# Products with the values on the two column halves of the array, each head with its own probabilities

## The chip, the core and the metric

The kernel runs on one core of a Trainium2 chip. The metric is device time in microseconds (us) from one launch to its end; lower is better. Before the change three runs gave 427.7, 428.08 and 429.15 us, median 428.08 us.

The core has TensorE (PE in the rows, with PEld for its weight loads), VectorE (DVE), ScalarE (ACT), GpSimd (POOL) and SyncE (SP), which issues the transfers. They run at the same time and wait for each other by semaphores.

## What is computed

The reference is attention with four sink positions and a window of 128, then two layers; the second layer's experts are only touched by tokens with a positive skip score.

```python
# q, k, v: 2 batches x 8 heads x 768 positions x 64
scores = scale * np.matmul(q, k.transpose(0, 1, 3, 2))
scores = np.where(is_sink | in_window, scores, -1e9)
a = np.exp(scores - scores.max(-1, keepdims=True))
a = a / (a.sum(-1, keepdims=True) + 1e-09)
x = np.matmul(a, v)               # 1536 tokens x 512, the products with the values
h = x @ w_in                      # 512 x 2048
g = np.where(h >= 1, h, np.where(h <= -1, 0, (h + 1) ** 2 / 4))
x = g @ w_out                     # 2048 x 512; then the skip layer
```

## The kernel before, in words

Work on attention goes by pairs of heads: 2 batches x 3 groups of 256 positions (`g` = 0, 1, 2) x 4 pairs of heads, so 24 pairs. A pair passes through these steps, each a function of the kernel: `trans_q` and `trans_k` (transposes of queries and keys), `score` (products of queries and keys, maximum on VectorE, exponential on ScalarE), `norm` (division by the sum), `ptrans` (the probabilities are transposed, 128x128 blocks, and copied to the tile `pth`, one half for each head, by ScalarE at L421), `ptrans_sinks` (the same for the sinks' probabilities, copied to `psk` by ScalarE at L430) and `av`, the products with the values.

`score` works with 64 rows of TensorE's array for each head (L366): the two heads' operands lie on partitions 0 to 63 and 64 to 127, and their results go to two banks of PSUM. All other matmuls before the change use the whole array.

`av` (L432 to L458) takes a block of 128 keys at a time. The stationary operand is 128 keys x 128 columns, the 64 columns of both heads side by side. The moving operand is the probabilities of both heads one after the other, up to 2 x 256 columns. So the result has, for each head's probabilities, the product with both heads' values, and half of it is used: rows 0 to 63 of the first 256 columns, and rows 64 to 127 of the second 256. These products are in full fp32, which the trace shows as two passes for each matmul. A pair with `g` = 0 has two such matmuls (512 and 256 columns), the others three (512, 256 and 256 columns) and one for the sinks from `psk` (512 columns, in the reduced format fp32r, one pass). Then ScalarE copies each head's half to `xh` (L456) and VectorE takes the rest into `xl` (L457), so that `xh` + `xl` hold the result for the fp32r matmuls that follow.

The first layer (`h_mm` at L471, `h_act`, `y_mm` at L516) begins while attention still runs: its matmuls are cut into pieces, and TensorE's order is written out by hand in the loop at L668. In each step a string such as `..a..A...Ps` sets it: a dot stands for pieces of the layer, `a` and `b` for scores, `P` and `s` for the transposes of probabilities, `A` for `av`. The order of VectorE's and ScalarE's instructions in this part is set by a scheduler when the program is built. Weights come in as raw words through SP and are converted on VectorE and ScalarE (L175 to L186) in the same stretch. After the last pair the rest of the layer runs (`behind`, L553), with everything ordered by hand, and then a short end that reads the skip scores.

Of the kernel before, what the change touches and what calls it, by code (L numbers as in the profile page):

```python
# [8 lines left out]
F32 = mybir.dt.float32  # L9
# [3 lines left out]
AF = mybir.ActivationFunctionType  # L13
ALU = mybir.AluOpType
# [10 lines left out]
def attention_moe_skip_kernel(  # L25
# [15 lines left out]
    nc = tc.nc  # L41
    B, H, S, D = q.shape
    NT, DM = out.shape
    DFF = w_in.shape[1]
    P = 128
# [53 lines left out]
    for i in range(2):  # L99
        a, b = mask[i][:, 0:P], mask[i][:, P + SK:]  # L100
# [4 lines left out]
    xh = [xp.tile([P, KC, 256], F32R, name=f"xh{g}") for g in range(NGRP)]  # L105
    xl = [xp.tile([P, KC, 256], F32R, name=f"xl{g}") for g in range(NGRP)]
# [9 lines left out]
    vall = ap.tile([P, 3, H, D], F32, name="vall", bufs=1)  # L116
# [5 lines left out]
    psk = ap.tile([P, 256], F32R, name="psk", bufs=1)  # L122


    kst, vsk = {}, {}
# [144 lines left out]
    def geo(n):  # L270

        b, g, h = units[n]
        return b, g, h, ([2 * g + 1, 2 * g] if g % 2 else [2 * g, 2 * g + 1]), (0 if g % 2 else 1)
# [158 lines left out]
    def av(u):  # L432
        b, g, h, _, _ = geo(2 * u)
        o = pst.tile([P, 512], F32, name="pt")


        oj = o.rearrange("p (j c) -> p j c", j=2)

        if g == 0:
            mm = [(1, 0, 256, 0), (2, 128, 128, 2)]  # L440
        else:
            mm = [(1, 0, 256, 0), (2 if g % 2 else 0, 0, 128, 2), (0 if g % 2 else 2, 128, 128, 3)]
        todo = []
        pth = pr_[u]["pth"]
        for kb, c0, w, i0 in mm:
            vs = vall[:, kb, h:h + 2].rearrange("p j d -> p (j d)")
            todo.append((oj[:, :, c0:c0 + w], vs, pth[:, :, i0 * P:i0 * P + w]))
        if g:
            todo.append((oj, vsk[b][:, h // 2], psk[0:72].unsqueeze(1).to_broadcast([72, 2, 256])))
        for i, (out_, lhs, rhs) in enumerate(todo):  # L450
            nc.tensor.matmul(out_, lhs, rhs, start=(i == 0), stop=(i == len(todo) - 1))  # L451
        gi = b * NG + g
        hp = h // 2
        for j in range(2):
            r = slice(D * j, D * j + D)
            nc.scalar.activation(xh[gi][r, hp], oj[r, j], AF.Copy)  # L456
            nc.vector.tensor_tensor(out=xl[gi][r, hp], in0=oj[r, j], in1=xh[gi][r, hp].bitcast(F32), op=ALU.subtract)  # L457
        pr_[u] = None  # L458


# [206 lines left out]
    with tc.manual_schedule(engines={mybir.EngineType.PE}):  # L667
        for s_ in range(-1, NU + 1):  # L668
# [26 lines left out]
            for what in order:  # L695
                if what == ".":
                    a, b = np_ * dot // dots, np_ * (dot + 1) // dots
                    dot += 1
                    for i in range(b - a):
                        pieces[done["piece"]]()  # L700
                        done["piece"] += 1
                elif what == "q":
                    upto("tq", done["tq"] + 1, NPR, trans_q)
                elif what == "k":
                    upto("tk", done["tk"] + 1, NPR, trans_k)
                elif what == "a" and s_ // 2 + 1 < NPR:
                    score(s_ // 2 + 1, 0)
                elif what == "b" and (s_ + 1) // 2 < NPR:
                    score((s_ + 1) // 2, 1)
                    norm((s_ + 1) // 2)  # L710
                elif what == "P":
                    upto("p", s_ + (s_ >= LAG), NU, ptrans)
                elif what == "s":
                    upto("ps", (s_ + (s_ >= LAG)) // 2, NPR, ptrans_sinks)
                elif what == "A":
                    upto("av", before // 2, NPR, av)
# [252 lines left out]
    todo = const.tile([P, NTT + 1], F32, name="todo")  # L969
# [45 lines left out]
```

## Time and profile before

| | |
|---|---|
| runs shown | 427.7, 428.08, 429.15 us |
| time of the profiled execution | 428.26 us |
| its span on the core | 426.4 us |
| mean granted clock of TensorE | 0.975 of full speed |
| busy: TensorE, its weight loads | 394.9 us (93%), 327.1 us (77%) |
| busy: VectorE, ScalarE, GpSimd | 267.0 us (63%), 231.5 us (54%), 30.5 us (7%) |
| moved by DMA | 53.29 MB, 125 GB/s on average |

The span runs from the first to the last instruction of the program; the execution's own time is 1.86 us longer. Busy time is an average over stretches with different limits, so the rows further down are taken stretch by stretch. A matmul's record lasts from its start to the modelled end of its results, which lies after the next matmul's start: the time that one takes of TensorE is the distance to the next start, not the length of its record.

### The profile page before, as it was taken

What the parts mean: (1) busy time and instruction counts of PE and PEld (TensorE: products, weight loads), DVE (VectorE), ACT (ScalarE), POOL (GpSimd) and SP (SyncE); (2) the same over time, 40 slices, a digit from 0 to 9 for tenths busy, and PEclk for the clock granted to TensorE, in tenths of its full rate; (3) what the DMA queues carried; (4) which work ended last, traced back from release to release, by engine and by line L of the source; (5) the groups of instructions that cost most, each with busy time, mean ns of one, the idle gap of its engine ahead of it and who ended that gap; (6) DMA issues with size and microseconds to landing.
All of it is one profiled execution on the core that took longest, in us unless ns stands there. A gap on an engine that the chain in (4) does not pass through costs nothing.

```text
span 426.4 us, 6940 instructions
## 1 busy us (share of the span) xinstructions
PE 394.9 (93%) x2420; PEld 327.1 (77%) x2420; DVE 267.0 (63%) x710; ACT 231.5 (54%) x563; POOL 30.5 (7%) x132
## 2 busy tenths in 40 slices
PE   4877869999999999999999899999999999999970
PEld 2544547777787787788789799999999999999960
DVE  1799974445566676555635987887837854444462
ACT  4788976666767676666664554554533333333310
POOL 5111110000001011100100000000000000000000
PEclk9988989999999999999999999999999999999995
DMA  8787561305033022100100656544435996555131
GB/s 191 193 244 203 160 199 26 73 2 138 10 78 101 16 62 72 53 22 7 49 2 25 198 180 216 148 119 128 141 105 180 312 321 214 184 188 187 48 137 69
DMA packets 65579, 53.29 MB, mean 125 GB/s; under 512 B 40320, under 2 KB 56704, under 8 KB 65536
## 3 DMA queue, kind: packets, MB, share of 16 engines
q1 hardware_dynamic: 64448, 52.51, 41.1%
q8 instruction: 21, 0.34, 0.3%
q10 hardware_dynamic: 1088, 0.26, 0.3%
q14 instruction: 22, 0.18, 0.1%
HBM read 46.47 MB, written 6.29 MB: 124 GB/s over the span
## 4 chain that ended last, share of the span: by engine, by line
PE 83%; DVE 4%; DMA 4%; issue 3%; ACT 2%; SPq 1%; POOL 1%; ACTq 0%; DVEq 0%; POOLq 0%
PE ph L471 20%; PE y L516 18%; PE z L516 11%; PE pt L471 11%; PE pt L451 9%; PE sc L366 5%; PE pt L417 4%; PE pt L304 1%; DMA ext<-in_window_dram 1%; DMA raw<-in_moe_w_in_dram 1%; DVE pr L370 1%; PE pt L331 1%; PE pt L429 1%; DMA out_dram<-mr 1%; DVE mr L539 1%
## 5 line engine op out<-in xcount | busy, mean ns | idle before, releaser
L471 PE MATMUL ph<-xh,wi 128*128 128x256 f32 x496 | 95.2, 290 | 4.2 <-DVE mt L491 3.6
L471 PEld LDWEIGHTS ph<-xh,wi 128*128 128x128 f32 x496 | 77.7, 189 | 9.1 <-DVE mt L491 3.9
L516 PE MATMUL y<-wo,gh 128*128 128x512 f32 x224 | 73.1, 408 | 1.2 <-ACT mr L535 1.2
L471 PE MATMUL ph<-xl,wi 128*128 128x256 f32 x248 | 70.0, 282 | 0.6 <-DVE xl L457 0.6
L374 ACT ACTIVATE pr<-pr,negmax 128x260 f32<-128x260 f32 (+1 forms) x96 | 46.8, 488 | 26.1 <-DVE negmax L370 25.4
L499 DVE TENSOR_TENSOR gl<-mt,gh 128x512 fp32r<-128x512 f32 x48 | 33.2, 692 | 27.5 <-ACT gh L493 27.2
L516 PE MATMUL z<-wo,gh 128*128 128x512 f32 x160 | 49.3, 389 | 0.0
L471 PE MATMUL pt<-xh,wi 128*128 128x256 f32 x272 | 48.8, 281 | 0.0
L493 ACT ACTIVATE gh<-mt 128x512 fp32r<-128x512 f32 x48 | 30.3, 630 | 33.5 <-DVE mt L491 12.2
L471 PEld LDWEIGHTS ph<-xl,wi 128*128 128x128 f32 x248 | 47.5, 192 | 0.8 <-DVE xl L457 0.8
L451 PE MATMUL pt<-pth,vall 128*128 128x256 f32 (+1 forms) x128 | 45.6, 491 | 1.4 <-ACT qtf L307 1.4
L516 PEld LDWEIGHTS y<-wo,gh 128*128 128x128 f32 x224 | 38.5, 189 | 8.0 <-ACT mr L535 1.4
L516 PE MATMUL y<-wo,gl 128*128 128x512 f32 x112 | 43.9, 392 | 0.0
L471 PEld LDWEIGHTS pt<-xh,wi 128*128 128x128 f32 x272 | 42.7, 188 | 1.3
L491 DVE SCALAR_TENSOR_TENSOR mt<-ph,mt 128x512 f32<-128x512 f32 x31 | 21.4, 689 | 28.6 <-ACT mt L486 28.4
L485 ACT ACTIVATE mt<-ph,half 128x512 f32<-128x512 f32 x31 | 21.2, 684 | 31.8 <-PE ph L471 31.6
L471 PE MATMUL pt<-xl,wi 128*128 128x256 f32 x136 | 38.2, 281 | 0.0
L451 PEld LDWEIGHTS pt<-pth,vall 128*128 128x128 f32 x128 | 24.5, 202 | 16.8 <-issue 13.2
L370 DVE CUSTOM_DVE_ANT_0 pr<-sc,mask 128x260 f32<-128x260 f32 x64 | 25.4, 424 | 16.3 <-PE sc L366 16.1
L457 DVE TENSOR_TENSOR xl<-pt,xh 64x256 fp32r<-64x256 f32 x48 | 20.2, 420 | 23.5 <-ACT xh L456 23.0
L516 PEld LDWEIGHTS z<-wo,gh 128*128 128x128 f32 x160 | 28.8, 188 | 4.9
L516 PE MATMUL z<-wo,gl 128*128 128x512 f32 x80 | 31.1, 389 | 0.0
(101 smaller groups left out, 617.0 us busy)
## 6 DMA issues: line engine op xcount, KB each, us to landing
raw<-in_moe_w_in_dram SPq DMA_DIRECT2D x32, 512.0 KB
raw<-in_moe_w_out_dram SPq DMA_DIRECT2D x32, 512.0 KB
vall<-in_v_dram SPq DMA_DIRECT2D x24, 128.0 KB
ypart<-mr SPq DMA_DIRECT2D x12, 256.0 KB
yi<-ypart SPq DMA_DIRECT2D x12, 256.0 KB
out_dram<-mr SPq DMA_DIRECT2D x12, 256.0 KB
qn<-in_q_dram SPq DMA_DIRECT2D x22, 128.0 KB
kn<-in_k_dram SPq DMA_DIRECT2D x22, 128.0 KB
```

The costliest lines, as they stand in the source:

```text
L366: nc.tensor.matmul(scs[j][:, :w], qq[r], kk[r], start=(n == 0), stop=(n == len(parts) - 1))
L370: nc.vector.tensor_tensor_reduce(out=a, in0=scs[j][:, :w], in1=m, scale=-0.125, scalar=BIG, op0=ALU.add, op1=ALU.min, accum_out=negmax[:, ...
L374: nc.scalar.activation(a, a, AF.Exp, bias=negmax[:, mi:mi + 1], scale=-1.0, accum_out=lsum[:, 2 * j + t:2 * j + t + 1])
L417: nc.tensor.transpose(pt[:, P * i:P * i + P], pr[:, t, c:c + P], ident)
L451: nc.tensor.matmul(out_, lhs, rhs, start=(i == 0), stop=(i == len(todo) - 1))
L457: nc.vector.tensor_tensor(out=xl[gi][r, hp], in0=oj[r, j], in1=xh[gi][r, hp].bitcast(F32), op=ALU.subtract)
L471: nc.tensor.matmul(ph, wih[f + i][:, wx, c * P:c * P + P], xx[gi][:, c], start=(c == 0 and x == 0), stop=(c == KC - 1 and x == 2),)
L485: nc.scalar.activation(t, ph, AF.Relu, bias=half, scale=0.5)
L491: nc.vector.scalar_tensor_tensor(out=t, in0=ph, scalar=1.0, in1=t, op0=ALU.max, op1=ALU.min)
L493: nc.scalar.activation(gh, t, AF.Copy)
L499: eng.tensor_tensor(out=gl, in0=t, in1=gh.bitcast(F32), op=ALU.subtract)
L516: nc.tensor.matmul(ycur[gi, tt], gg[:, c:c + P], woh[f + i][:, wx], start=(u == us[0] and i == 0 and x == 0), stop=(u == us[-1] and i == 1 ...
```

## The change

`av` alone changes. The sinks' product comes first, with the whole array and the 256 columns of `psk` once, since both heads' rows of `psk` and of `vsk` lie apart anyway. Each product with a block of keys is cut into two matmuls: the stationary operand is one head's 64 columns, the moving operand that head's probabilities alone, and the result goes to rows 0 to 63 or 64 to 127 of the same 256 columns. Such a matmul uses 64 columns of the array, the first head the left half and the second the right half. One copy on ScalarE and one subtraction on VectorE, both over 128 rows, take the place of two each. After the change `av` is at L443 to L452, and later lines have moved up by five.

```diff
-        oj = o.rearrange("p (j c) -> p j c", j=2)
-
         if g == 0:
             mm = [(1, 0, 256, 0), (2, 128, 128, 2)]
         else:
             mm = [(1, 0, 256, 0), (2 if g % 2 else 0, 0, 128, 2), (0 if g % 2 else 2, 128, 128, 3)]
-        todo = []
         pth = pr_[u]["pth"]
-        for kb, c0, w, i0 in mm:
-            vs = vall[:, kb, h:h + 2].rearrange("p j d -> p (j d)")
-            todo.append((oj[:, :, c0:c0 + w], vs, pth[:, :, i0 * P:i0 * P + w]))
         if g:
-            todo.append((oj, vsk[b][:, h // 2], psk[0:72].unsqueeze(1).to_broadcast([72, 2, 256])))
-        for i, (out_, lhs, rhs) in enumerate(todo):
-            nc.tensor.matmul(out_, lhs, rhs, start=(i == 0), stop=(i == len(todo) - 1))
+            nc.tensor.matmul(o[:, 0:256], vsk[b][:, h // 2], psk[0:72], start=True, stop=False)
+        for i, (kb, c0, w, i0) in enumerate(mm):
+            for j in range(2):
+                nc.tensor.matmul(
+                    o[D * j:D * j + D, c0:c0 + w], vall[:, kb, h + j], pth[:, j, i0 * P:i0 * P + w],
+                    start=(i == 0 and g == 0), stop=(i == len(mm) - 1))
         gi = b * NG + g
         hp = h // 2
-        for j in range(2):
-            r = slice(D * j, D * j + D)
-            nc.scalar.activation(xh[gi][r, hp], oj[r, j], AF.Copy)
-            nc.vector.tensor_tensor(out=xl[gi][r, hp], in0=oj[r, j], in1=xh[gi][r, hp].bitcast(F32), op=ALU.subtract)
+        nc.scalar.activation(xh[gi][:, hp], o[:, 0:256], AF.Copy)
+        nc.vector.tensor_tensor(out=xl[gi][:, hp], in0=o[:, 0:256], in1=xh[gi][:, hp].bitcast(F32), op=ALU.subtract)
```

TensorE's order around a pair with sinks, late in attention, before the change:

```order
L366 MATMUL sc<-kt_145,qt 128x260 x6
L516 MATMUL y_2095<-wo,gh 128x512 x2
L516 MATMUL y_2095<-wo,gl 128x512
L451 MATMUL pt<-pth,vall 128x512
L451 MATMUL pt<-pth,vall 128x2x128 x2
L451 MATMUL pt<-psk,vsk 128x512
L471 MATMUL ph<-xh_128,wi 128x256 x2
L471 MATMUL ph<-xl_134,wi 128x256
```

And after it:

```order
L366 MATMUL sc<-kt_145,qt 128x260 x6
L511 MATMUL y_2105<-wo,gh 128x512 x2
L511 MATMUL y_2105<-wo,gl 128x512
L443 MATMUL pt<-psk,vsk 128x256
L446 MATMUL pt<-pth,vall 64x256 x2
L446 MATMUL pt<-pth,vall 64x128 x4
L466 MATMUL ph<-xh_128,wi 128x256 x2
L466 MATMUL ph<-xl_134,wi 128x256
```

What stands before and behind the pair is the same; the sinks' product moved from the end to the front, and three matmuls over the whole array became six over half of it. Whole-array matmuls stand on both sides.

ScalarE's order at the end of the same part of the program, before the change (`xh` is the copy in question, `psk` the sinks' copy, `mt` and `gh` belong to the layer):

```order
L374 ACTIVATE pr,lsum<-pr,negmax 128x260 x2
L486 ACTIVATE mt<-mt 128x512
L456 ACTIVATE xh_128<-pt 64x256
L493 ACTIVATE gh<-mt 128x512
L456 ACTIVATE xh_128<-pt 64x256
L421 ACTIVATE pth<-pt 128x512
```

And after it:

```order
L374 ACTIVATE pr,lsum<-pr,negmax 128x260 x2
L481 ACTIVATE mt<-mt 128x512
L451 ACTIVATE xh_128<-pt 128x256
L421 ACTIVATE pth<-pt 128x512
L488 ACTIVATE gh<-mt 128x512
```

The second copy is gone, and the copy of the next pair's probabilities has moved ahead of `gh`. Elsewhere too the scheduler has put VectorE's and ScalarE's instructions in another order, most in the first pairs.

## Rows read from the trace of the kernel before

**Rows 1.** Three stretches: length, busy time of PE, PEld, DVE, ACT, POOL, clock, DMA:

```profile
20.00:62.00 42.00, 31.59 (x148) 20.09 (x147) 37.87 (x106) 36.79 (x104) 6.33 (x18) 0.90 0.72 213
62.00:226.00 164.00, 163.40 (x1026) 129.07 (x1026) 92.40 (x319) 106.37 (x302) 16.92 (x78) 0.99 0.18 47
226.00:414.00 188.00, 186.36 (x1201) 169.63 (x1199) 124.59 (x243) 76.29 (x122) 0.00 (x0) 1.00 0.52 168
```

**Rows 2.** Two of these stretches, L451 alone: busy time of PE and PEld:

```profile
20.00:62.00 42.00, 10.06 (x23) 4.50 (x21) 0.90 0.72 213
62.00:226.00 164.00, 38.49 (x121) 22.46 (x121) 0.99 0.18 47
```

**Rows 3.** Timeline of TensorE around one pair with sinks (start us, length us):

```profile
188.09 0.28 PE L471 MATMUL ph<-xh,wi 128*128 128x256 f32 x1
...
188.67 1.88 PE L451 MATMUL pt<-pth,vall 128*128 128x512 f32 x6
...
190.63 0.64 PE L516 MATMUL y<-wo,gh 128*128 128x512 f32 x2
```

**Rows 4.** Timeline of TensorE, single passes of one pair without sinks:

```profile
136.54 0.59 PE L451 MATMUL pt<-pth,vall 128*128 128x512 f32 x1
...
136.97 0.38 PE L451 MATMUL pt<-pth,vall 128*128 128x256 f32 x1
...
137.19 0.38 PE L451 MATMUL pt<-pth,vall 128*128 128x256 f32 x1
```

**Rows 5.** Timeline of TensorE, transposes and a visit of `score` in fp32, in parts:

```profile
30.70 0.49 PE L417 MATMUL pt<-ident,pr 128*128 128x128 f32 x3
...
30.92 0.27 PE L417 MATMUL pt<-ident,pr 128*128 128x128 f32 x1
...
31.12 0.49 PE L366 MATMUL sc<-ktf,qtf 64*128 64x260 f32 x2
...
31.44 0.39 PE L366 MATMUL sc<-ktf,qtf 64*128 64x260 f32 x2
```

**Rows 6.** Timeline of TensorE, a visit whose second head came late:

```profile
33.15 0.48 PE L366 MATMUL sc<-ktf,qtf 64*128 64x260 f32 x1 [0.84 <-DVE negmax L370]
...
33.48 0.51 PE L366 MATMUL sc<-ktf,qtf 64*128 64x260 f32 x2
```

**Rows 7.** Timeline of TensorE, from a visit of `score` to the whole array:

```profile
46.28 0.39 PE L366 MATMUL sc<-ktf,qtf 64*128 64x260 f32 x2
...
46.60 0.50 PE L471 MATMUL ph<-xh,wi 128*128 128x256 f32 x2
...
46.82 0.28 PE L471 MATMUL ph<-xh,wi 128*128 128x256 f32 x1
```

**Rows 8.** Groups by shape, 64 and 128 rows: busy, mean ns of one, idle before:

```profile
L456 ACT ACTIVATE xh<-pt 64x256 fp32r<-64x256 f32 x48 | 18.1, 378 | 17.8 <-PE pt L451 9.7 <-DVE xl L457 7.5
L336 ACT ACTIVATE kt<-pt 128x256 fp32r<-128x256 f32 x12 | 4.5, 374 | 0.0
L457 DVE TENSOR_TENSOR xl<-pt,xh 64x256 fp32r<-64x256 f32 x48 | 20.2, 420 | 23.5 <-ACT xh L456 23.0
L337 DVE TENSOR_TENSOR kt<-pt,kt 128x256 fp32r<-128x256 f32 x12 | 5.1, 421 | 2.7 <-ACT kt L336 2.7
```

**Rows 9.** Timeline of TensorE, its waits between 49 and 60 us:

```profile
50.45 0.50 PE L471 MATMUL ph<-xh,wi 128*128 128x256 f32 x2 [0.57 <-ACT xh L456]
51.51 0.39 PE L471 MATMUL ph<-xl,wi 128*128 128x256 f32 x1 [0.56 <-DVE xl L457]
...
59.26 0.50 PE L471 MATMUL ph<-xh,wi 128*128 128x256 f32 x2 [3.62 <-DVE mt L491]
```

**Rows 10.** Timeline of all engines, the sinks' copy `psk` and the start of `av`:

```profile
187.15 0.37 ACT L430 ACTIVATE psk<-pt 72x256 fp32r<-72x256 f32 x1
...
215.16 0.36 ACT L430 ACTIVATE psk<-pt 72x256 fp32r<-72x256 f32 x1
...
215.36 1.07 PE L451 MATMUL pt<-pth,vall 128*128 128x512 f32 x2
```

## The prediction

> **What bounds the kernel now.** I read busy time by stretches first, since the busy share of the whole span mixes them. From 62 to 226 us, where attention and the first layer are interleaved, TensorE is busy 163.4 of 164 us, ScalarE 106.4 and VectorE 92.4; from 226 to 414 us it is 186.4 of 188. In both TensorE is the bound, and what it is spared shortens the time. From 20 to 62 us it is not: TensorE is busy 31.6 of 42 us, VectorE 37.9, ScalarE 36.8 [rows 1]. The same stretches for line 451 alone tell where the changed products lie: 121 passes between 62 and 226 us [rows 2]. A pair with sinks has seven passes (two for each of three fp32 matmuls, one for the sinks), one without has four, and 15 x 7 + 4 x 4 = 121: 15 pairs with sinks and 4 without lie where TensorE is the bound. The other 5 of the 24 (4 without, 1 with) lie earlier.
>
> Then the timeline, pass by pass. A pass over 512 columns takes 0.43 us (136.54 to 136.97), one over 256 columns 0.22 [rows 4]; so 0.43 for 512, 0.215 for 256 and, in proportion, 0.108 for 128. A pair with sinks goes from 188.67 to the next line's start at 190.63, 1.96 us [rows 3]: two passes at 0.43 and four at 0.215 are 1.72, which leaves 0.24 for the sinks. A pair without them is 2 x 0.43 + 2 x 0.215 = 1.29 us.
>
> **The change, part by part.** *The columns.* Each fp32 product now streams half the columns, but there are twice as many matmuls, so TensorE gains only if the two heads' matmuls run side by side. No row shows two matmuls side by side on column halves. The nearest rows are `score`, which has the two heads on row halves. There the two first passes of the two heads fill 31.12 to 31.61 together and the second passes start at 31.44: each pass pair takes about as long as one pass alone, 0.22 us for 260 columns [rows 5]. I take the same for column halves. Then a pair without sinks streams 2 x (0.215 + 0.108) = 0.645 us, one with sinks 2 x (0.215 + 0.108 + 0.108) = 0.86. The bounds are these and no sharing at all, 1.29 and 1.72 us.
>
> On columns only the skill has a figure: the Trainium skill's page TensorE: Matmul & The Clock Gate (Part 3, Measured speedup vs the span model) gives 2.38 times for three column tiles; an estimate from it, 79% of the ideal, is 1.59 times for two, 1.08 us instead of 0.86, and the whole sum 421 us.
>
> *The sinks.* One pass over 256 columns in fp32r. The layer's passes of that size and format stand 0.12 us apart (five between 188.09 and 188.67 [rows 3]); so 0.12 instead of 0.24.
>
> *Changing between the whole array and halves.* This is what the change adds. Before a visit of `score` the last of three transposes starts at 30.92, and each takes (0.49 - 0.27) / 2 = 0.11 us, so its columns end at 31.03; the second passes start at 31.44, so the first ones' columns began at 31.22. That is 0.19 us with nothing streaming [rows 5]. Leaving a visit, the last passes start at 46.28 and end their columns at 46.50; the next pass but one starts at 46.82, and 0.12 before it, at 46.70, the first one's columns began: 0.20 us [rows 7]. `av` has whole-array matmuls on both sides, as the order shows, and the sinks' product, whole too, stands ahead of the halves, so each of the 24 pairs pays both once: 0.39 us. Column halves may cost less (first weight load of 64 columns) or more; bounds nothing and twice as much. I take the rows as they are.
>
> Sum for TensorE: a pair with sinks 0.12 + 0.39 + 0.86 = 1.37, which is 0.59 less than 1.96. One without 0.39 + 0.645 = 1.03, 0.26 less than 1.29. In the bound stretch 15 x 0.59 + 4 x 0.26 = 9.9 us.
>
> *One copy and one subtraction.* A copy of 64 x 256 takes 378 ns on ScalarE, one of 128 x 256 374; on VectorE 420 and 421 [rows 8]. Twice the rows cost nothing more, so each pair spares 0.38 us of ScalarE and 0.42 of VectorE. From 62 us on this hides behind TensorE and counts as nothing. TensorE's saving needs that cover too: if it takes 9.9 us less for the stretch, about 154 us remain, and ScalarE keeps 106 - 19 x 0.38 = 99 of work in them. Before 62 us the two engines are close to full, and 5 pairs spare VectorE 2.1 us and ScalarE 1.9. TensorE also waits there for exactly these halves, 0.57 us for `xh` and 0.56 for `xl` [rows 9]. But the scheduler has written both engines' order anew in this stretch, and transfers take part in it (DMA busy 0.72). I count half of 2.1, 1.0 us; bounds 2.5 gained (all of it, and a little of the waits) and 3.6 lost (a new wait like the longest there, the 3.62 us at 59.26 [rows 9]).
>
> *A wait moved.* The sinks' product now stands first, so `av` waits for `psk` about 1.7 us sooner; queued behind it are the pair's other products and then the layer's pieces. `psk` was ready at 187.52 for the pair at 188.67, but at 215.52 for the one that began at 215.36 [rows 10, 3]. I count 0.2 us once. The products' own wait for `pth` is the same as before, since ScalarE writes `pth` ahead of `psk`.
>
> The rest of the program is the same work from attention's end on, bound by TensorE, and moves up as a whole. The profiled execution took 428.26 us, 0.2 above the median of the runs shown; 428.26 - 9.9 - 1.0 + 0.2 = 417.6 us.
>
> **The rivals.**
>
> *Side by side, but in the order of the program.* Each fp32 matmul is two passes. If a matmul may not start ahead of one that stands before it, head 1's first pass waits for head 0's second to start, and only these two overlap. Worked through, with passes of 0.215 and 0.108 us, the streams end 0.215 us later in both kinds of pairs (0.86 instead of 0.645, 1.08 instead of 0.86). 19 x 0.215 = 4.1 us are lost: 421.7 us. Against it: in `score` the first two passes start together, so head 1's first pass went ahead of head 0's second [rows 5]; and where head 1 came late, head 0's first pass ran alone and its second shared the array with head 1's first [rows 6]. For it: rows show this for row halves alone. The page named above says in the same Part 3 (What overlaps and what doesn't) that matmuls start and end in strict program order; by that rule this rival would be the forecast, and the two rows on `score` disagree with it.
>
> *No side by side.* Column halves need two different moving operands on all 128 partitions at once; row halves need one on each set of 64, so the rows on `score` do not prove it. If the halves run one after the other, a pair with sinks takes 0.12 + 0.39 + 1.72 = 2.23 us, 0.27 more than before, and one without 0.39 + 1.29 = 1.68, 0.39 more: 15 x 0.27 + 4 x 0.39 = 5.6 us. With the 1.0 spared earlier and the 0.2 added, 433.1 us. It turns slower than before once the two heads share less than about 0.3 of the 1.72 us, which is what the changes of the array and the shorter sinks come to.
>
> *The first stretch gives part of it back.* If the new order on VectorE and ScalarE adds one wait of 3.6 us before 62 us in place of the 1.0 spared, the time is 428.26 - 9.9 + 0.2 + 3.6 = 422.2 us. For it: waits of this size stand in that stretch now. Against it: less work on the two engines that are full there.
>
> **How the numbers follow.** The forecast 0.66, order of the program 0.12, no side by side 0.11, the first stretch 0.11. About 0.3%, 1.3 us, is what can be told from no change. The forecast and the order rival are faster; the first stretch is, but for 0.03, where its waits eat the whole gain; no side by side is slower. So faster 0.86, same 0.03, slower 0.11. The forecast's own range is 414 to 420, from 2.5 us gained before 62 us and somewhat cheaper changes of the array to about 2 lost. With changes of the array that cost nothing 19 x 0.39 = 7.4 us more would be gained, with twice the cost as much lost; part of that, and both faster rivals, set the range at 412 to 425 us. It leaves out the slower case.
>
> **What would show it.** In the changed profile: the two heads' first passes at the new products start within some 10 ns of each other; a pair with sinks takes about 1.37 us from the sinks' start to the next line's start and one without 1.03; TensorE stays above 99% busy until attention ends, now near 215 us; one copy and one subtraction a pair at 0.37 and 0.42 us. The prediction is wrong if head 1's passes begin only when head 0's have ended, if much more than 0.39 us of a pair passes with nothing streaming, or if attention's first part ends later than 62 us.

## The result and the profile after

The changed kernel takes 416.28 us (median of four runs, 414.88 to 417.27), the kernel before 428.21 (427.7 to 429.15): a ratio of 0.971, 95% interval 0.969 to 0.974. Forecast was 417.6 us. The profiled execution took 416.49 us against 428.26, 11.8 us less.

First the stretches. The columns are as in [rows 1]: length, busy time of PE, PEld, DVE, ACT and POOL, clock, DMA. Each boundary lies 0.3 to 0.4 us ahead of the sixth pair's start, 3.3 us behind the last pair's start, and at the end of the layer, as in [rows 1].

```profile
20.00:60.20 40.20, 28.63 (x170) 18.63 (x167) 35.55 (x102) 34.17 (x99) 6.30 (x19) 0.85 0.77 229
60.20:215.20 155.00, 153.69 (x1136) 121.27 (x1136) 84.10 (x301) 98.16 (x283) 16.88 (x78) 0.99 0.20 50
215.20:402.40 187.20, 185.68 (x1197) 169.00 (x1196) 123.81 (x242) 76.17 (x121) 0.00 (x0) 1.00 0.52 168
```

Against [rows 1] the middle stretch is 9.0 us shorter (164.0 to 155.0), and TensorE is still busy for all but 1.3 us of it. The first is 1.8 us shorter, the last 0.8. The middle one ends a fixed time behind the last pair's start, so what the last pair itself gains, some 0.6 us, falls into the last stretch here. The granted clock of the middle stretch is the same 0.99.

Now one pair with sinks on TensorE, in the place of [rows 3]: start, length, then the line. The last three rows are parts of the second `av` row, cut out by narrow windows.

```profile
179.75 0.28 PE L466 MATMUL ph<-xl,wi 128*128 128x256 f32 x1
179.87 0.28 PE L443 MATMUL pt<-psk,vsk 72*128 72x256 f32 x1
180.08 1.09 PE L446 MATMUL pt<-pth,vall 128*64 128x256 f32 x12
181.10 0.73 PE L511 MATMUL y<-wo,gh 128*128 128x512 f32 x2
181.67 0.40 PE L511 MATMUL y<-wo,gl 128*128 128x512 f32 x1
...
180.08 0.44 PE L446 MATMUL pt<-pth,vall 128*64 128x256 f32 x2
...
180.34 0.39 PE L446 MATMUL pt<-pth,vall 128*64 128x256 f32 x2
...
180.56 0.50 PE L446 MATMUL pt<-pth,vall 128*64 128x128 f32 x6
```

Two passes fill 180.08 to 180.52 together, where one takes 0.43; the next two start together at 180.34, and those of 128 columns follow from 180.56. That is the picture of `score` in [rows 5], on columns instead of rows. The 12 passes cover 1.09 us with the tail of the last.

The row behind the pair, and its weight loads (PEld), tell when TensorE really goes on:

```profile
181.10 0.30 PEld L511 LDWEIGHTS y<-wo,gh 128*128 128x128 f32 x2 [0.17 <-issue]
```

The second pass at L511 starts at 181.10 + 0.73 - 0.39 = 181.44 and the one behind it at 181.67, so a pass takes 0.23 us, and the first one's columns began 0.23 before the second's, at 181.21. The second load starts there too (181.10 + 0.30 - 0.19). So the pair takes 1.34 us from the sinks' start (179.87) to 181.21, where it took 1.96. Its parts: sinks 0.12; then nothing streams until 180.13 (0.215 ahead of the second passes at 180.34), 0.14 us; columns until 181.00, 0.87 us; and 0.20 us until 181.21.

On the other engines a copy and a subtraction over 128 rows take what those over 64 took [rows 8], 24 of each in place of 48 (busy, mean ns, idle before):

```profile
L452 DVE TENSOR_TENSOR xl<-pt,xh 128x256 fp32r<-128x256 f32 x24 | 10.1, 420 | 12.1 <-ACT xh L451 12.0
L451 ACT ACTIVATE xh<-pt 128x256 fp32r<-128x256 f32 x24 | 9.0, 376 | 5.3 <-PE pt L446 5.1
```

The waits of TensorE between 47 and 58 us, in the place of those of [rows 9]:

```profile
47.99 0.38 PE L443 MATMUL pt<-psk,vsk 72*128 72x256 f32 x1 [1.25 <-ACT psk L430]
...
57.24 0.50 PE L466 MATMUL ph<-xh,wi 128*128 128x256 f32 x2 [3.21 <-DVE mt L486]
```

The two waits for `xh` and `xl` are gone, the long one for `mt` has stayed, and a new one for `psk` stands ahead of the fifth pair, since the sinks' product now comes first.

### The profile page after: what moved, and what is told of

Read it like the earlier page. It is cut to its first block, busy times and chain, and to the rows that moved or that the text cites. A ratio compares the mean times of both kernels' runs of the same rounds, so it can differ in the third digit from the quotient of the medians.

```text
span 414.7 us, 7132 instructions
## 1 busy us (share of the span) xinstructions
PE 381.2 (92%) x2548; PEld 316.9 (76%) x2548; DVE 255.5 (62%) x686; ACT 220.5 (53%) x539; POOL 30.2 (7%) x132
## 4 chain that ended last, share of the span: by engine, by line
PE 78%; DVE 8%; ACT 5%; DMA 4%; issue 2%; SPq 1%; POOL 0%; ACTq 0%; DVEq 0%
PE ph L466 20%; PE y L511 18%; PE z L511 12%; PE pt L466 11%; PE sc L366 6%; PE pt L446 4%; PE pt L417 3%; ACT pr L374 2%; PE pt L304 2%; DMA ext<-in_window_dram 1%; DMA raw<-in_moe_w_in_dram 1%; DVE pr L370 1%; DVE mt L486 1%; PE pt L331 1%; PE pt L429 1%
## 5 line engine op out<-in xcount | busy, mean ns | idle before, releaser
L466 PEld LDWEIGHTS ph<-xh,wi 128*128 128x128 f32 x496 | 76.9, 189 | 10.1 <-DVE mt L486 4.0
L511 PE MATMUL y<-wo,gh 128*128 128x512 f32 x224 | 73.7, 410 | 1.3 <-ACT mr L530 1.3
L511 PE MATMUL z<-wo,gh 128*128 128x512 f32 x160 | 49.3, 389 | 0.0
L511 PEld LDWEIGHTS y<-wo,gh 128*128 128x128 f32 x224 | 37.7, 188 | 9.2 <-issue 2.4
L511 PE MATMUL y<-wo,gl 128*128 128x512 f32 x112 | 43.9, 392 | 0.0
L421 ACT ACTIVATE pth<-pt 128x512 f32<-128x512 f32 (+1 forms) x48 | 26.7, 557 | 15.4 <-PE pt L417 15.3
L511 PEld LDWEIGHTS z<-wo,gh 128*128 128x128 f32 x160 | 28.8, 188 | 4.8
L417 PE MATMUL pt<-ident,pr 128*128 128x128 f32 x176 | 29.1, 285 | 2.9 <-ACT pr L389 1.7
L511 PE MATMUL z<-wo,gl 128*128 128x512 f32 x80 | 31.1, 389 | 0.0
L481 ACT ACTIVATE mt<-mt 128x512 f32<-128x512 f32 x48 | 30.3, 632 | 1.1
```

The costliest lines, as they stand in the source:

```text
L417: nc.tensor.transpose(pt[:, P * i:P * i + P], pr[:, t, c:c + P], ident)
L421: nc.scalar.activation(pr["pth"][:, n % 2, :w], pt[:, :w], AF.Copy)
L466: nc.tensor.matmul(ph, wih[f + i][:, wx, c * P:c * P + P], xx[gi][:, c], start=(c == 0 and x == 0), stop=(c == KC - 1 and x == 2),)
L481: nc.scalar.activation(t, t, AF.Square)
L511: nc.tensor.matmul(ycur[gi, tt], gg[:, c:c + P], woh[f + i][:, wx], start=(u == us[0] and i == 0 and x == 0), stop=(u == us[-1] and i == 1 ...
```

## The experiments

Each kernel is the changed kernel with one edit, or two where the text says so. Times are medians; a ratio is to the kernel before, run beside it on the same chip, with its 95% interval. The kernel before had medians of 429.33 us beside e1 to e4, 428.94 beside e5 to e7, 429.18 beside e8 to e11 and 428.78 beside e12, all somewhat above the 428.21 beside the change; so ratios are the better comparison between groups. Two numbers from each trace tell where the time lies: when the sixth pair with its products began (the end of the first stretch), and how long it was from there to the start of the last pair.

| kernel | us | ratio (interval) | sixth pair at | from there to the last pair |
|---|---|---|---|---|
| before | 428.21 | 1 | 62.3 | 160.3 |
| the change | 416.28 | 0.971 (0.969 to 0.974) | 60.6 | 151.4 |
| the change again (e11) | 417.11 | 0.971 (0.970 to 0.973) | 60.5 | 151.9 |
| e1 two copies | 423.30 | 0.986 (0.982 to 0.989) | 65.1 | 153.1 |
| e2 whole array | 428.64 | 0.998 (0.995 to 1.001) | 64.5 | 159.1 |
| e3 one half | 435.14 | 1.014 (1.010 to 1.018) | 62.6 | 167.2 |
| e4 head by head | 423.32 | 0.987 (0.982 to 0.992) | 61.3 | 157.0 |
| e5 sinks between | 421.89 | 0.986 (0.983 to 0.988) | 61.1 | 155.4 |
| e6 next to scores | 412.98 | 0.965 (0.962 to 0.967) | 59.1 | 147.4 |
| e7 sinks last | 416.72 | 0.973 (0.970 to 0.975) | 59.4 | 151.5 |
| e8 two copies, sinks last | 422.91 | 0.985 (0.983 to 0.987) | 65.2 | 153.1 |
| e9 whole array, same loads | 428.32 | 0.998 (0.997 to 0.999) | 64.2 | 159.4 |
| e10 one copy, two subtractions | 418.50 | 0.975 (0.974 to 0.977) | 60.5 | 152.1 |
| e12 two copies, one subtraction | 423.54 | 0.986 (0.984 to 0.989) | 67.3 | 151.1 |

**e3: nothing side by side.**

```diff
-                    o[D * j:D * j + D, c0:c0 + w], vall[:, kb, h + j], pth[:, j, i0 * P:i0 * P + w],
+                    o[0:D, 256 * j + c0:256 * j + c0 + w], vall[:, kb, h + j], pth[:, j, i0 * P:i0 * P + w],
...
+            nc.scalar.activation(xh[gi][r, hp], oj, AF.Copy)
```

> As the change, but both heads on the left column half, their results beside each other in rows 0 to 63 (so two copies and two subtractions, and the sinks in two passes of 64 columns). Nothing can run side by side. Theory: a pair with sinks takes 0.35 + 2 x 0.12 + 1.72 = 2.3 us in place of 1.34 and one without 1.64 in place of 0.99: 15 x 0.97 + 4 x 0.65 = 17 us more than the change and 1 to 2 us for the copies, 434 us. Rival (narrow matmuls are cheaper in themselves, side by side or not): 420 us or less.

Measured 435.14 us, slower than before by 1.4% (interval 1.0 to 1.8%), as the theory had it. In its trace a pair's first passes are single:

```profile
185.18 0.43 PE L448 MATMUL pt<-pth,vall 128*64 128x256 f32 x1
...
185.44 0.38 PE L448 MATMUL pt<-pth,vall 128*64 128x256 f32 x1
...
185.18 1.95 PE L448 MATMUL pt<-pth,vall 128*64 128x256 f32 x12
187.06 0.50 PE L471 MATMUL ph<-xh,wi 128*128 128x256 f32 x2
```

The same 12 passes, 64 columns of the array each, cover 1.95 us instead of 1.09. So narrow matmuls are no cheaper in themselves; running side by side is what the change lives on, and without it the rival of the prediction that ends slower than before is what happens.

**e4: all of head 0 first.**

```diff
-        for i, (kb, c0, w, i0) in enumerate(mm):
-            for j in range(2):
+        for j in range(2):
+            for i, (kb, c0, w, i0) in enumerate(mm):
```

> As the change, but all of head 0's products are issued before head 1's. Theory (each column half takes its own matmuls as they come, and TensorE reaches past at least six waiting passes): no difference, 416.3 us, within 0.5. Rival (only the neighbour in the program's order can overlap): the halves run one after the other but for one pass, up to 15 x 0.75 + 4 x 0.43 = 13 us more, 427 to 429 us.

Measured 423.32 us, between the two: both fell. The trace tells a limit. In a pair without sinks (four passes a head) both heads start together, and it costs what it did (0.81 us to the next line's start, 0.80 in the change). In a pair with sinks (six passes a head) head 1 is late:

```profile
132.85 0.44 PE L446 MATMUL pt<-pth,vall 128*64 128x256 f32 x2
```

```profile
175.74 0.43 PE L446 MATMUL pt<-pth,vall 128*64 128x256 f32 x1
...
176.01 0.65 PE L446 MATMUL pt<-pth,vall 128*64 128x256 f32 x3
...
175.74 1.57 PE L446 MATMUL pt<-pth,vall 128*64 128x256 f32 x12
```

The first fence is a pair without sinks: two passes at once, though three passes of head 0 still wait ahead of head 1's first. The second is one with sinks: at 175.74 head 0's first pass runs alone, and the third pass that joins the row from 176.01 is head 1's first, at 176.23 (176.01 + 0.65 - 0.43), when head 0's third has started and three of its passes are left. So here TensorE takes a pass for the idle half past three waiting ones, but not past four or five. Counted in matmuls of two passes it is one that waits and not two; these rows can't tell the two ways of counting apart. The 12 passes cover 1.57 us. The rule of strict program order that the prediction weighed as a rival does not hold for these halves: head 1's first matmul runs ahead of matmuls of head 0 that were issued before it. The order of issue still matters.

**e5: four changes of the array instead of two.**

```diff
-        if g:
-            nc.tensor.matmul(o[:, 0:256], vsk[b][:, h // 2], psk[0:72], start=True, stop=False)
...
+            if g and i == 0:
+                nc.tensor.matmul(o[:, 0:256], vsk[b][:, h // 2], psk[0:72], start=False, stop=False)
```

> As the change, but the sinks' whole-array product stands between the first and the second block of keys, so a pair with sinks changes between whole array and halves four times instead of two. Theory (a way in and a way out cost 0.35 us together, as the trace of the change shows): 15 x 0.35 = 5.2 us more, 421.5 us. Rival (the gaps are the engine filling and emptying once a pair, whatever the modes): 417 us or less.

Measured 421.89 us, 4.8 more than the change in e11 by the medians, 6.2 by the ratios (0.986 and 0.971), and 5.2 more than e7, which ran beside it and is as fast as the change; the theory had 5.2. A pair in its trace:

```profile
183.05 0.28 PE L466 MATMUL ph<-xl,wi 128*128 128x256 f32 x1
183.26 0.65 PE L444 MATMUL pt<-pth,vall 128*64 128x256 f32 x4
183.84 0.38 PE L448 MATMUL pt<-psk,vsk 72*128 72x256 f32 x1
184.15 0.66 PE L444 MATMUL pt<-pth,vall 128*64 128x128 f32 x8
184.74 0.73 PE L511 MATMUL y<-wo,gh 128*128 128x512 f32 x2
```

From the end of the layer's columns (183.05 + 0.12 = 183.17) to the next columns (184.74 + 0.11) it is 1.68 us, against 1.34: a way in and a way out cost 0.34 us together, and the price is for the change, not for the pair.

**e6 and e7: one change fewer.** e7 only puts the sinks' product last; e6 also moves the scores' visit next to it.

```diff
+        if g:
+            nc.tensor.matmul(o[:, 0:256], vsk[b][:, h // 2], psk[0:72], start=False, stop=True)
...
-            order = ("aAPs", "bqkAPs", "..a..A...Ps", "..b.qk.APs.")[s_ % 2 + 2 * (s_ >= 9)]
+            order = ("aAPs", "bqkAPs", "....aA...Ps", "..b.qk.APs.")[s_ % 2 + 2 * (s_ >= 9)]
```

> As the change, with the sinks' product last again and nothing else. It tells how much of the run beside it is due to the sinks' place. Theory (the earlier wait for psk costs 0.2 us, and the scheduler's order moves the first stretch by some tenths): 415.5 to 416.8 us. Rival (the waits for psk cost something in many pairs): 415 us or less.

> As the change, but the sinks' product last, and the scores' visit (row halves) moved to stand right ahead of av (column halves), so that in the second part of attention a step has three changes of the array instead of four. Theory (each change costs about 0.2 us, whichever two ways of using the array it is between): 19 x 0.17 = 3.3 us less, 413 us. Rival one (from row halves to column halves costs as much as the two changes it replaces): 416.3 us. Rival two (the scores come later, and TensorE waits for the exponentials): 418 us or more.

e7 took 416.72 us, as its theory said: the sinks' place is worth nothing that can be told. e6 took 412.98 us, a ratio of 0.965 (0.962 to 0.967), 3.7 less than e7 beside it and the best of all here; the theory said 413. The step in its trace:

```profile
174.51 0.62 PE L366 MATMUL sc<-kt,qt 64*128 64x260 f32 x6
175.06 1.09 PE L444 MATMUL pt<-pth,vall 128*64 128x256 f32 x12
176.08 0.39 PE L448 MATMUL pt<-psk,vsk 72*128 72x256 f32 x1
...
175.06 0.65 PE L444 MATMUL pt<-pth,vall 128*64 128x256 f32 x4
```

The scores' last passes start at 174.51 + 0.62 - 0.28 = 174.85 and end their columns 0.12 later, at 174.97. The second passes of the halves start at 175.06 + 0.65 - 0.38 = 175.33, so the first ones' columns began at 175.11: 0.14 us from row halves to column halves, no more than from the whole array. It replaces a way out (0.20) and a way in (0.14), which spares 0.20 us. 18 pairs stand behind the scores, 17 of them from the sixth on, and 17 x 0.20 = 3.4 us. The stretch from the sixth to the last pair is 4.1 us shorter than e7's, and 0.7 of that is the clock: e7's begins with 1.3 us at 1.2 GHz, the lower of the two levels, and e6's does not.

**e1, e8, e10, e12: the merged copy and subtraction.** The edit of e1 stands first; e8 adds that of e7. Behind it are the lines of e10 and of e12 in place of the changed kernel's two.

```diff
-        nc.scalar.activation(xh[gi][:, hp], o[:, 0:256], AF.Copy)
-        nc.vector.tensor_tensor(out=xl[gi][:, hp], in0=o[:, 0:256], in1=xh[gi][:, hp].bitcast(F32), op=ALU.subtract)
+        for j in range(2):
+            r = slice(D * j, D * j + D)
+            nc.scalar.activation(xh[gi][r, hp], o[r, 0:256], AF.Copy)
+            nc.vector.tensor_tensor(out=xl[gi][r, hp], in0=o[r, 0:256], in1=xh[gi][r, hp].bitcast(F32), op=ALU.subtract)
```

```diff
 # e10
+        nc.scalar.activation(xh[gi][:, hp], o[:, 0:256], AF.Copy)
+        for j in range(2):
...
+            nc.vector.tensor_tensor(out=xl[gi][r, hp], in0=o[r, 0:256], in1=xh[gi][r, hp].bitcast(F32), op=ALU.subtract)
 # e12
+        for j in range(2):
...
+            nc.scalar.activation(xh[gi][r, hp], o[r, 0:256], AF.Copy)
+        nc.vector.tensor_tensor(out=xl[gi][:, hp], in0=o[:, 0:256], in1=xh[gi][:, hp].bitcast(F32), op=ALU.subtract)
```

> The changed kernel with two copies and two subtractions of 64 rows a pair again; the products stay on the column halves. Theory (the halved columns on TensorE carry the gain, the merged copy only helps before 62 us): 1.0 to 1.8 us are given back, 417.3 to 418.1 us against 416.3 for the change. Rival (the shorter way from av to xh and xl carries half of the gain or more): 422 us or more.

> Two copies and two subtractions a pair as in e1, the sinks' product last as in e7; the products on the column halves. It undoes the merged copy a second time, under another order of VectorE's and ScalarE's queues, since e1's loss of some 6 us lay before 66 us. Theory (the second copy and subtraction themselves cost the first stretch 4 to 6 us, well above the 2.1 us that they last): 421 to 423 us. Rival (the copies cost 1 to 2 us, and e1 had an unlucky order of the queues besides): 417.5 to 419 us.

> The change with one copy and two subtractions of 64 rows a pair: VectorE has its 0.42 us a pair again, ScalarE is spared. Theory (VectorE is the fuller engine of the first stretch, so its second subtraction is what counts): 419 to 422 us. Rival (ScalarE's second copy is what holds it): 417.5 us or less.

> The change with two copies of 64 rows and one subtraction a pair: ScalarE has its 0.38 us a pair again, VectorE is spared. With e10 it tells whose second instruction made e1 and e8 reach the sixth pair at 65 us and not at 60.5. Theory (ScalarE's second copy, which stands in its queue ahead of the next probabilities): the sixth pair at 64 to 65 us, 421 to 423 us. Rival (neither alone; the first stretch depends on how the scheduler happens to order the queues): the sixth pair at 60 to 62 us, 417 to 419 us.

> The change itself once more, to stand beside the other runs on the same chip. Every theory: 416.3 to 417.5 us, 0.971 of the kernel before.

e1 took 423.30 us where I expected 417.3 to 418.1: the theory fell by its number, and the rival's number (422 or more) came true. But not in the way that the rival meant: from the sixth pair on e1 is 1.2 to 1.7 us behind the change's two traces and its pairs take the same 1.23 us; 4.5 us are lost before the sixth pair. e8, with the sinks last, shows the same (65.2). e10 gives VectorE its second subtraction back and the sixth pair stays at 60.5; the run is 1.4 us above the change beside it, less than the theory's 2 to 5 and a little more than the rival's. e12 gives ScalarE its second copy back, and the sixth pair comes at 67.3, later even than its theory's 64 to 65; its 423.54 us are near what was expected, since the middle stretch is a little shorter. So with both column halves in use the three kernels with ScalarE's second copy reach the sixth pair 4.5 to 7 us later than the change, and VectorE's second subtraction alone makes no difference there. Rows on `psk`, first the change, then e1, then e12 (the rows are of one kernel each):

```profile
60.56 0.41 PE L443 MATMUL pt<-psk,vsk 72*128 72x256 f32 x1
```

```profile
50.49 0.58 PE L443 MATMUL pt<-psk,vsk 72*128 72x256 f32 x1 [1.89 <-ACT psk L430]
...
65.07 0.41 PE L443 MATMUL pt<-psk,vsk 72*128 72x256 f32 x1
```

```profile
42.64 1.30 PE L417 MATMUL pt<-ident,pr 128*128 128x128 f32 x4 [3.70 <-ACT pr L389]
...
53.13 0.39 PE L443 MATMUL pt<-psk,vsk 72*128 72x256 f32 x1 [2.83 <-ACT psk L430]
...
67.29 0.28 PE L443 MATMUL pt<-psk,vsk 72*128 72x256 f32 x1
```

The sixth pair begins at 60.56, 65.07 and 67.29. TensorE waits longer for `psk` in the two kernels with two copies, 1.89 and 2.83 us against 1.25, and in e12 3.70 for the division at L389.

That these waits make up the delay is not shown. The granted clock differs too. Here is the stretch from 20 us to the sixth pair (columns as in [rows 1]) in the change, in e11, in e1 and in e12, one kernel each:

```profile
20.00:60.50 40.50, 28.93 (x171) 18.93 (x168) 35.85 (x102) 34.30 (x99) 6.30 (x19) 0.85 0.76 228
```

```profile
20.00:60.60 40.60, 30.59 (x172) 19.94 (x168) 35.97 (x102) 34.41 (x99) 6.11 (x19) 0.90 0.77 226
```

```profile
20.00:65.00 45.00, 34.38 (x171) 22.61 (x168) 38.67 (x108) 36.46 (x103) 6.55 (x19) 0.80 0.71 203
```

```profile
20.00:67.20 47.20, 32.92 (x171) 21.16 (x170) 36.33 (x103) 37.30 (x105) 5.70 (x19) 0.86 0.66 196
```

In e1 TensorE is idle for 45.00 - 34.38 = 10.6 us, no longer than in the change (11.6 and 10.0 in e11). It is busy for longer, 34.4 us against 28.9 and 30.6 over as many matmuls, at a clock of 0.80 against 0.85 and 0.90. In e12 it is both idle for longer, 14.3 us, and busy for longer, 32.9. Ahead of 50.40 in e1, where the wait of 1.89 us lies, TensorE was busy for 1.61 of 3.40 us; the next 6.8 us were granted 0.50 of the clock, 1.2 GHz:

```profile
47.00:50.40 3.40, 1.61 (x11) 1.05 (x10) 3.25 (x10) 3.34 (x9) 1.81 (x5) 1.00 0.67 184
50.40:57.20 6.80, 6.71 (x31) 5.48 (x33) 4.93 (x11) 4.02 (x11) 0.00 (x0) 0.50 0.56 174
```

So the lower clock is a rival to the second copy as the cause, or a link between the two. It goes with the kernel and not with the chance of one run: over all runs the mean clock of the whole span has a median of 0.964 to 0.969 in e1, e8, e9 and e12 and of 0.972 or more in every other kernel. It is not the whole account either: e2, late as well, has 0.973, and the change reached the sixth pair at the same time with 0.85 and with 0.90 of the clock in this stretch. No run separates the two.

**e2 and e9: the merged copy without the halves.** The values stand in 128 columns with zeros for the other head, so both heads add into the same 256 columns on the whole array. e2 loads them with twice as many transfers, e9 with as many as before.

```diff
-                    o[D * j:D * j + D, c0:c0 + w], vall[:, kb, h + j], pth[:, j, i0 * P:i0 * P + w],
+                    o[:, c0:c0 + w], vall[:, kb, h + j], pth[:, j, i0 * P:i0 * P + w],
...
+    nc.vector.memset(vall, 0.0)
...
 # e9: one transfer for both heads of each pair
+            nc.sync.dma_start(
+                vall[:, s0 + t, h0 // 2:h0 // 2 + 2].rearrange("p n (j y) -> p (n j) y", j=2)[:, :, 0:D],
...
```

> One copy and one subtraction a pair as in the change, but the products on the whole array: each head's values stand in 128 columns of which the other head's 64 are zero, so both heads add into the same 256 columns, one head after the other. Columns streamed as before the change, no change between whole array and halves, sinks 256 columns. Theory: gains 15 x 0.12 = 1.8 us for the sinks and 1.0 to 1.8 us before 62 us: 424.5 to 425.5 us. Rival (copies carry the gain): 419 us or less.

> e2 once more (whole array, values padded with zeros, one copy and one subtraction), with the values loaded by as many transfers as in the kernel before; e2 had twice as many, and its first stretch ended 2 us later than before. Theory (the merged copy helps the first stretch whatever the products do): 62 us is reached 1 to 3 us earlier than before, and with 1.7 us for the sinks the time is 424 to 426 us. Rival (the merged copy gives nothing by itself): 427 us or more.

Both theories fell: 428.64 and 428.32 us; e9's lies in the range of its rival, 427 or more. From the sixth pair on e9 gains 0.9 us, half of the 1.7 expected of the sinks; but the sixth pair comes at 64.2, 1.8 later than before, in spite of one copy. The transfers, which I suspected in e2, were not it, or not all of it: with as many as before, only 0.4 us of e2's delay went. Both kernels also set the padding to zero on VectorE at the start (2.6 us in e2, 1.3 in e9), but e9 begins its first pair only 0.3 us later than the kernel before (19.5 and 19.2), so most of its delay arises behind that. Its clock from 20 us to the sixth pair is 0.79, against 0.90 before; so e9 does not show that the merged copy is worth nothing.

So the first stretch is not a sum. Whole array and two copies end it at 62.3, whole array and one copy at 64.2, halves and two copies at 65 to 67 (but 62.6 in e3, with both heads on one half), halves and one copy at 59 to 61 (seven traces: the change twice, e4 to e7, e10). Each has its own order of ScalarE's and VectorE's queues and its own granted clock. What in these costs the 2 to 7 us stays open: no run held the order or the clock fixed while the work changed.

## Why the prediction was right, step by step

- *Side by side on column halves*, taken from row halves without a row for columns: right. The columns of a pair with sinks take 0.87 us where 0.86 was forecast; e3 is the counter-proof, and its 2.31 us a pair (184.85 to 187.06, and 0.10 until columns stream; it has the sinks twice) are within a tenth of the 2.23 of the rival. The prediction's other estimate, 1.08 us, is off by 0.21; its whole sum should have read 421.5 us, 15 x 0.22 + 4 x 0.17 = 4.0 above the forecast.
- *Changes of the array*, 0.39 us a pair: 0.34 in the trace and in e5. The way in was the part that was too dear, 0.14 us instead of 0.19.
- *A pair*: 1.37 us forecast, 1.34 measured with sinks. In "what would show it" I set 1.37 to the next line's start; by the rows this is 1.23, since the next matmul's record begins 0.11 us before its columns. Without sinks 1.03 was forecast; 129.51 to 130.51 is 1.00 (the row below with 0.11 added; the line ahead of it ended its columns at 129.39 + 0.12).

```profile
129.39 0.28 PE L466 MATMUL ph<-xl,wi 128*128 128x256 f32 x1
129.60 0.87 PE L446 MATMUL pt<-pth,vall 128*64 128x256 f32 x8
130.40 0.73 PE L511 MATMUL y<-wo,gh 128*128 128x512 f32 x2
```

- *The stretch bound by TensorE*: 9.9 us forecast for 19 pairs; by the measured prices 15 x 0.62 + 4 x 0.29 would be 10.5. Measured between the same two events, the sixth pair's first product and the first matmul of the layer's part behind attention, it became (225.98 - 62.34) - (214.67 - 60.56) = 9.5 us shorter. The rows are before, then after; the row at 60.56 stands further up:

```profile
62.34 2.72 PE L451 MATMUL pt<-pth,vall 128*128 128x512 f32 x6
...
225.98 0.40 PE L471 MATMUL pt<-xh,wi 128*128 128x256 f32 x2
```

```profile
214.67 0.40 PE L466 MATMUL pt<-xh,wi 128*128 128x256 f32 x2
```

The trace tells where the difference to 10.5 went. Taken from the matmul ahead of a pair to the second one behind it, most pairs save 0.62 or 0.29 us, as they should. Two save only 0.04 and 0.15, since TensorE then waits for `mt`, and the second of them for `psk` as well:

```profile
138.69 0.47 PE L466 MATMUL ph<-xh,wi 128*128 128x256 f32 x2 [0.46 <-DVE mt L486]
...
204.60 0.40 PE L511 MATMUL y<-wo,gl 128*128 128x512 f32 x1
205.04 0.39 PE L443 MATMUL pt<-psk,vsk 72*128 72x256 f32 x1
...
206.60 0.39 PE L466 MATMUL ph<-xh,wi 128*128 128x256 f32 x1 [0.15 <-DVE mt L486]
```

The pair at 60.56 saves more, 0.92; it ran in part at 1.2 GHz, like the one at 62.34 before. All 19 pairs come to 10.1 us, and between the pairs 0.6 are lost. So the term was right to 0.4 us because two errors nearly cancel: a pair saves a little more than forecast, and other engines become the limit for moments once TensorE is spared, which the sum left out.

- *The first stretch*: 1.0 us forecast, 1.8 measured. The number was near, the reason was not. I took it from VectorE's time; e10 shows that VectorE's second subtraction alone is worth nothing there; in e1, e8 and e12, with ScalarE's second copy, the stretch is several us longer, at a lower clock in e1 and e8, and which of the two does it is open. In e1 and e8, the halves without the merged copy, it is 2.8 us longer than before, within the bound of 3.6 that I gave to a new order of the queues. That this term came out near is luck.
- *The wait for `psk`*: 0.2 us forecast for the pair that began at 215.36. There it came true: the pair's place is now 205.04, 0.44 us behind the matmul at 204.60, where a pass takes 0.23. But a dearer one came that was not foreseen, 1.25 us ahead of the fifth pair, in the first stretch, where it is part of the 1.8 that were gained on balance. e7, without the wait, reaches the sixth pair 1.2 us sooner, but the whole time is the same.

The sum was 10.7 us, 11.8 were measured: 1.8 in the first stretch (1.0 forecast), 9.5 in the second, waits included (9.7), and 0.5 behind attention and outside the span, where nothing was forecast. That the total is so near owes something to errors of both signs. The rival of program order, 421.7 us, is 5.2 us off the profiled execution; the rows show both heads' passes starting together at 180.08. One reading in the prediction was too strong: at the visits of `score` only the passes of the two heads interleave, while the heads' matmuls, two passes each, still start and end in program order. So those rows spoke against the rival as it was worked through, by passes; that whole matmuls can pass each other was first shown by e4.

## What to carry to other kernels

Where half of a matmul's result is thrown away, two matmuls on the halves of the array can run side by side, if they are issued in turn; here two passes took the time of one. Reckon with a price for each change of the array, here 0.14 us into halves and 0.20 out, and put the visits to halves next to each other. Merging two copies into one is free when they differ only in rows, but its worth in a stretch where several engines are nearly full can't be read from the duration of the copy. There, compare when the same event comes in both traces, and the granted clock up to it, before giving a gain to one edit.

## What the runs showed of the hardware that I had not expected

- TensorE took a pass for the free half past three waiting passes of the other half, but not past four (e4; in matmuls, past one but not past two).
- The granted clock went with the kernel: the medians over all runs, for the whole span, are 0.964 to 0.969 in e1, e8, e9 and e12 and 0.972 or more in the others.
- From row halves straight to column halves there were 0.14 us with nothing streaming, as from the whole array, so two kinds of halves next to each other save a whole way out (e6).
- Two fp32r matmuls of 64 columns of the array, one after the other on the same half, stand 0.12 us apart, as whole ones do: 184.85 and 184.97 in e3, in the row of both below.

```profile
184.85 0.40 PE L444 MATMUL pt<-psk,vsk 72*64 72x256 f32 x2
```
